# Talking-heads attention and two expert layers on one core: the raw mixing weights are cleared by VectorE and loaded first

## The chip, the cores and the metric

The kernel runs on one core of a Trainium2 chip. The metric is device microseconds from start to end of one execution; a lower number is better. A core has five engines that take their instructions in order, each from its own list: TensorE (PE; its weight loads are shown apart as PEld), VectorE (DVE), ScalarE (ACT), GpSimd (POOL) and SyncE (SP). In this kernel transfers are issued by SP and, for a few, by ACT; the transfer engines behind them are shared.

## The reference

Three stages follow each other. Only the first one is near the change.

```python
# q, k, v: 4 x 12 x 448 x 64; w_pre, w_post: 12 x 12
scores = scale * np.matmul(q, k.transpose(0, 1, 3, 2))
scores = np.einsum('bhij,hg->bgij', scores, w_pre)      # mixes the 12 heads
attn = softmax(scores)
attn = np.einsum('bhij,hg->bgij', attn, w_post)         # mixes them again
attn_out = np.matmul(attn, v)
# then: x of 1792 x 768; h = x @ w_in; x = (h - tanh(h)) @ w_out
# then: a soft mixture of 8 experts with 4 slots each, weights w1 and w2
```

## The kernel before, in words

**Attention.** Four batches are cut into chunks of at most 120 query rows, 16 chunks in all, and each chunk into slots of up to 10 query rows, which are worked on two at a time. For a chunk, PE transposes q, multiplies it by the transposed keys of each pair of heads (`sc`, line 283), ACT and DVE copy the scores to a tile `S`, and SP regroups them by a transfer `D<-S` (line 308) so that the 12 heads of 10 query rows lie on the partitions. One matmul by the block matrix `wpre` (line 317) mixes the heads. Exponentials, sums, the second mixing (line 360) by a scaled copy of the block matrix `wpost` and the product with v (line 399) follow. The later layers begin when attention ends.

**The order of the work.** It is written out by hand: every engine gets its instructions in the order in which the program names them, and only the waits between engines are added. Before the loop over slots there is a prologue. SP loads the six pairs of heads of k for the first batch (`kn`, line 166) and the first chunks of q (`qn`, line 179). PE spends the wait on ten matmuls on the identity (`warm`, line 538). Then for each pair of heads p, PE transposes k to `kx` (line 240), ACT rounds it to `khi` (line 245), DVE computes the remainder `klo` (line 249), and from p = 2 on PE does the scores of pair p - 2. Two buffers hold `kx`, so the transposes of pair p + 2 wait for `klo` of pair p. The first q is treated alike (`qx`, `qT`, lines 262 to 266).

**The mixing matrices.** `kron` builds `wpre` and then `wpost`. Each call clears a tile (`wprer` or `wpostr`) on GpSimd (line 184), lets ACT issue the transfers that repeat the 12 x 12 weights down the partitions (line 186: one transfer of 120 rows for `wpre`, two of 60 rows for `wpost`, rows of 48 bytes), and then has GpSimd spread them and mask them to a block diagonal (lines 196 to 211). After that GpSimd clears the edges of other tiles (lines 531 to 536).

**Transfer semaphores.** Transfers of both queues take eight completion semaphores in turn (`DMAHW0` to `DMAHW7` below). A transfer that takes a semaphore again waits until the transfer that held it before has landed.

Of the kernel before, what the change touches and what calls it, by code (L numbers as in the profile page):

```python
# [16 lines left out]
NB, NH, SEQ, HD = 4, 12, 448, 64  # L17
# [4 lines left out]
IH = 5  # L22
# [109 lines left out]
def talking_heads(tc, ident, q, k, v, w_pre, w_post, xd, box, follow):  # L132
    nc = tc.nc
# [26 lines left out]
    def load_k(b, p):  # L160
        if b:
            t = er.tile([JP, NR, 2, HD], FP32, tag="kn", name="kn", bufs=NP)
            nc.sync.dma_start(out=t, in_=k[b, 2 * p:2 * p + 2].rearrange("e (p r) d -> p r e d", r=NR))
        else:
            t = er.tile([JP, 2, NR, HD], FP32, tag="kn", name="kn", bufs=NP)
            nc.sync.dma_start(out=t, in_=k[b, 2 * p:2 * p + 2].rearrange("e (p r) d -> p e r d", r=NR))
        nat_k[b, p] = t
# [8 lines left out]
    def load_q(n):  # L176
        b, i0, ni, _ = chunks[n]
        t = er.tile([CHUNK, NH, HD], FP32, tag="qn", name="qn")
        nc.sync.dma_start(out=t[:ni], in_=q[b, :, i0:i0 + ni, :].rearrange("h p d -> p h d"))
        nat_q[n] = t  # L180

    def kron(name, w, scale, pre):
        rep = lt.tile([128, NH], FP32, tag=name + "r", name=name + "r", bufs=1)
        nc.gpsimd.memset(rep, 0.0)
        for at_row, n in ((4, 2 * IH),) if pre else ((4, IH), (68, IH)):
            nc.scalar.dma_start(
                out=rep[at_row:at_row + n * NH], in_=w.unsqueeze(0).to_broadcast([n, NH, NH]))
        if pre:
            big = lt.tile([128, 2 * IH, NH], FP32, tag="big", name="big", bufs=2)
            src = rep.unsqueeze(1).to_broadcast([128, 2 * IH, NH])  # L190
            pat = [[NH, 2 * IH], [0, NH]]
        else:
            big = lt.tile([128, 2, NH, IH], FP32, tag="big", name="big", bufs=2)
            src = rep.unsqueeze(1).unsqueeze(3).to_broadcast([128, 2, NH, IH])
            pat = [[64, 2], [0, NH], [NH, IH]]
        nc.gpsimd.tensor_scalar(out=big, in0=src, scalar1=scale, scalar2=None, op0=ALU.mult)
        nc.gpsimd.affine_select(
            out=big, in_=big, pattern=[[-z, c] for z, c in pat], compare_op=ALU.is_ge, fill=0.0, base=-4,
            channel_multiplier=1)
        nc.gpsimd.affine_select(  # L200
            out=big, in_=big, pattern=pat, compare_op=ALU.is_ge, fill=0.0, base=NH + 3, channel_multiplier=-1)
        if pre:
            m = lt.tile([128, 64], FP32, tag=name, name=name, bufs=1)
            nc.gpsimd.memset(m, 0.0)
            for x in range(2):
                nc.gpsimd.tensor_copy(
                    out=m[64 * x:64 * x + 64, 4:], in_=big[64 * x:64 * x + 64, IH * x:IH * x + IH].rearrange("p i g -> p (i g)"))
        else:
            m = lt.tile([128, NH, IH], FP32, tag=name, name=name, bufs=1)
            for x in range(2):  # L210
                nc.gpsimd.tensor_copy(out=m[64 * x:64 * x + 64], in_=big[64 * x:64 * x + 64, x])
        return m
# [214 lines left out]
    def plan(kind, s, *a):  # L427
        at.setdefault((kind, s), []).append(a)
# [16 lines left out]
    for m in range(1, NC):  # L445
        w = len(chunks[m - 1][3])
# [11 lines left out]
    for m in range(1, NC):  # L458
        if chunks[m][1] + CHUNK >= SEQ and m + 1 < NC:
            w = len(chunks[m - 1][3])  # L460
# [51 lines left out]
    for hi, lo, cost, f, a in sorted(wanted, key=lambda z: (z[0] - z[1], z[0])):  # L512
        s = min(range(lo, hi + 1), key=crowd)
        load["dma"][s] += cost
        plan("load", s, f, *a)

    load_k(0, 0)
    load_q(0)
    for p in (1, 2):
# [1 line left out]
    ds = [lt.tile([128, SEQ], FP32, tag=f"D{i}", name="D", bufs=1) for i in range(DB)]  # L521
    et = [lt.tile([128, SEQ + 64 - JH], FP32, tag=f"e{i}", name="e", bufs=1) for i in range(2 * EB)]
    vns = [lt.tile([128, NP, NR, HD], FP32, tag=f"vn{i}", name="vn", bufs=1) for i in range(3)]
    wpre = kron("wpre", w_pre, HD ** -0.5, True)
    wpost = kron("wpost", w_post, 1.0, False)
    warm = ps.tile([128, 128], FP32, tag="t", name="warm", bufs=2)

    for p in range(3, NP):
# [851 lines left out]
def fused_kernel(  # L1380
# [56 lines left out]
    with tc.manual_schedule():  # L1437
        talking_heads(
            tc, ident, q, k, v, w_pre, w_post, xd, box,
            lambda: moe_and_slots(tc, ident, xd, wi, wo, wo4, wis, (tshift, tlimit, moe2_phi, sel, sela, seld), moe2_w1, moe2_w2, out, box))  # L1440
# [29 lines left out]
```

## Time and profile before

| | us |
|---|---|
| median of 3 runs | 914.09 |
| lowest and highest | 909.67 and 916.29 |
| the profiled execution | 910.57 |
| span in its profile, first to last instruction | 908.8 |

| engine | busy us | share of the span |
|---|---|---|
| PE | 830.0 | 91% |
| ACT | 573.5 | 63% |
| DVE | 559.3 | 62% |
| POOL | 256.6 | 28% |

The profile is of one execution. Busy time is an average over stages that have different limits, so a stage is read by the view that follows the chain of waits back from the last instruction. Times are counted from the first instruction. The granted clock is a share of TensorE's full speed: 1.00 is 2.4 GHz and 0.50 is 1.2 GHz.

### The profile page before, as it was taken

How to read it: one execution, taken by the hardware profiler on the slowest of the kernel's cores; microseconds unless marked ns; L12 is line 12 of the kernel's file. 1: busy time of each engine (PE TensorE's matmuls, PEld its weight loads, DVE VectorE, ACT ScalarE, POOL GpSimd, SP SyncE). 2: the span in 40 equal slices, each digit the busy share in tenths (PEclk: the TensorE clock that was granted, in tenths of full speed). 3: DMA queues.
4: the chain of work that ended last, by engine and by line, in shares of the span. 5: the costliest groups of instructions: out<-in, count | busy, mean ns of one | idle time of the engine just before them, and what ended most of it. 6: DMA issues, size and time to landing. Idle time of an engine off the chain costs nothing.

```text
span 908.8 us, 28664 instructions
## 1 busy us (share of the span) xinstructions
PE 830.0 (91%) x11750; PEld 591.5 (65%) x11750; DVE 559.3 (62%) x1183; ACT 573.5 (63%) x1351; POOL 256.6 (28%) x440
## 2 busy tenths in 40 slices
PE   7868999889998899889979999999999999999995
PEld 5535676566765667666668777767776776875553
DVE  2446878668787687877445566657766777740104
ACT  2756888668877688888656676546664666731113
POOL 5334345434454344544302322000000015600000
PEclk8989999999999999999989999999999999998998
DMA  5699898897989878885648968578854435979998
GB/s 110 177 210 226 239 234 247 227 243 218 243 244 228 243 229 240 250 242 189 195 169 279 329 225 273 213 300 327 310 208 174 155 124 194 324 313 425 426 372 308
DMA packets 145910, 224.53 MB, mean 247 GB/s; under 512 B 60852, under 2 KB 127476, under 8 KB 142196
## 3 DMA queue, kind: packets, MB, share of 16 engines
q1 hardware_dynamic: 142432, 209.83, 73.8%
q10 hardware_dynamic: 3348, 12.87, 3.6%
q8 instruction: 93, 1.52, 0.7%
q14 instruction: 37, 0.30, 0.1%
HBM read 147.96 MB, written 36.18 MB: 203 GB/s over the span
## 4 chain that ended last, share of the span: by engine, by line
PE 68%; DMA 12%; ACT 8%; DVE 6%; issue 3%; POOL 1%; SPq 1%; ACTq 0%; POOLq 0%; DVEq 0%
PE hp L813 25%; DMA D<-S 9%; PE pm L317 7%; PE sc L283 6%; PE vx L399 6%; PE tm L360 6%; DVE mx L321 3%; ACT e L329 3%; PE h L1255 3%; PE gt L884 3%; PE so L1296 2%; PE tz L1275 2%; DMA rg<-wi 2%; PE lgp L934 2%; PE sp L1016 1%
## 5 line engine op out<-in xcount | busy, mean ns | idle before, releaser
L329 ACT ACTIVATE e<-pm,mx 128x448 f32<-128x448 f32 x184 | 115.1, 631 | 87.8 <-DVE mx L321 85.6
L360 PEld LDWEIGHTS tm<-wk,e 64*64 64x64 f32 x5888 | 118.2, 137 | 61.5 <-issue 37.9
L813 PE MATMUL hp<-xa,rg 128*128 128x512 f32 x576 | 152.4, 404 | 0.0
L321 DVE TENSOR_REDUCE mx<-pm 128x1 f32<-128x448 f32 x184 | 106.0, 617 | 68.8 <-PE pm L317 68.6
L360 PE MATMUL tm<-wk,e 64*64 64x60 f32 x5888 | 127.3, 223 | 17.8 <-issue 10.3
L317 PE MATMUL pm<-D,wpre 64*64 64x448 f32 (+2 forms) x736 | 119.2, 570 | 20.1 <-DMA D<-S 15.9
L813 PEld LDWEIGHTS hp<-xa,rg 128*128 128x128 f32 x576 | 102.4, 188 | 28.6 <-issue 10.8
L291 ACT ACTIVATE S<-sc 120x448 f32<-120x448 f32 (+1 forms) x186 | 91.4, 551 | 10.5 <-PE sc L283 6.6
L346 POOL TENSOR_SCALAR wk<-wpost,rv 128x60 f32<-128x60 f32 x184 | 88.4, 502 | 16.6 <-DVE rv L339 13.4
L283 PE MATMUL sc<-khi,qT 64*120 64x448 f32 (+1 forms) x384 | 84.6, 396 | 7.7 <-DVE xs L409 5.2
L775 POOL TENSOR_TENSOR rg<-rg 128x384 fp32r<-128x384 f32 x32 | 32.0, 1011 | 205.9 <-DVE rg L772 192.0
L335 POOL TENSOR_SCALAR rv<-ss 128x2 f32<-128x2 f32 x92 | 26.0, 283 | 225.0 <-ACT e L329 185.4
L399 PE MATMUL vx<-aT,vn 128*64 128x120 f32 (+1 forms) x1536 | 85.9, 266 | 0.5 <-issue 0.4
L844 DVE SCALAR_TENSOR_TENSOR qd<-qd,sq 128x512 f32<-128x512 f32 (+1 forms) x62 | 38.3, 618 | 69.8 <-ACT mk L840 63.3
L399 PEld LDWEIGHTS vx<-aT,vn 128*64 128x64 f32 x1536 | 75.6, 139 | 6.9 <-issue 2.8
L833 ACT ACTIVATE sq<-hp 128x512 f32<-128x512 f32 (+1 forms) x62 | 32.8, 530 | 71.9 <-PE hp L813 71.9
L374 ACT ACTIVATE aT<-tm 128x480 f32<-128x480 f32 x144 | 75.8, 593 | 0.2 <-PE tm L360 0.2
L813 PE MATMUL hp<-xb,rg 128*128 128x512 f32 x288 | 74.7, 404 | 0.0
L70 POOL TENSOR_TENSOR fa<-fa,f 128x384 f32<-128x384 f32 x64 | 67.3, 1052 | 9.7 <-DVE rv L339 3.6
L317 PEld LDWEIGHTS pm<-D,wpre 64*64 64x64 f32 (+2 forms) x736 | 26.3, 132 | 61.8 <-DMA D<-S 24.6
L813 PEld LDWEIGHTS hp<-xb,rg 128*128 128x128 f32 x288 | 52.0, 188 | 16.6 <-issue 6.3
L283 PEld LDWEIGHTS sc<-khi,qT 64*120 64x120 f32 (+1 forms) x384 | 46.5, 175 | 25.0 <-PE tm L360 7.4
(185 smaller groups left out, 1394.2 us busy)
## 6 DMA issues: line engine op xcount, KB each, us to landing
ex<-in_moe_w_dram SPq DMA_DIRECT2D x25, 1536.0 KB
D<-S SPq DMA_DIRECT2D x144, 210.0 KB
rg<-wis SPq DMA_DIRECT2D x32, 768.0 KB
f<-in_moe_w_in_dram SPq DMA_DIRECT2D x32, 384.0 KB
f<-in_moe_w_out_dram SPq DMA_DIRECT2D x32, 384.0 KB
wis<-rg ACTq DMA_DIRECT2D x16, 768.0 KB
rg<-wi SPq DMA_DIRECT2D x26, 384.0 KB
wi<-fa SPq DMA_DIRECT2D x32, 192.0 KB
```

What stands on the lines that cost most here:

```text
L70: eng.tensor_tensor(out=out, in0=bits(a), in1=bits(p), op=ALU.add)
L283: nc.tensor.matmul(xs[e][0][:ni], lhsT=qT[n][s, l, p, :ni], rhs=kt[s], start=(i == 0), stop=(i == 2))
L291: nc.scalar.activation(out=dst, in_=xs[e][0][:ni], func=ACTF.Copy)
L317: nc.tensor.matmul(xs[x][64 * i:64 * i + 64], lhsT=wpre[k0:k1], rhs=d[i][k0:k1], start=True, stop=True)
L321: nc.vector.tensor_reduce(out=mx[:, x:x + 1], in_=xs[x], op=ALU.max, axis=AX.X, negate=True)
L329: nc.scalar.activation(out=es[x][:, :SEQ], in_=xs[x], func=ACTF.Exp, bias=mx[:, x:x + 1], accum_out=ss[:, x:x + 1])
L346: nc.gpsimd.tensor_scalar(out=wk, in0=wpost, scalar1=rv[:, x:x + 1], scalar2=None, op0=ALU.mult)
L360: nc.tensor.matmul(xs[i][64 * z:64 * z + 64, x, c], lhsT=es[x][h, j:j + 64], rhs=wks[x][h], start=True, stop=True)
L374: nc.scalar.activation(out=out[:, :, c0:c0 + m].rearrange("p a (x i) -> p a x i", x=2), in_=x, func=ACTF.Copy)
L399: nc.tensor.matmul(x[64 * e:64 * e + 64, i, :ni], lhsT=nat_v[b, h // NP][:, h % NP, c, :], rhs=a[:, c, h, :ni], start=(c == 0), stop=(c == ...
L813: nc.tensor.matmul(hp, lhsT=r32(w[:, m, hl, cs]), rhs=r32(x_of(b, c, l)), start=(c == 0 and i == 0), stop=(c == KD - 1 and i == 2))
L844: nc.vector.scalar_tensor_tensor(out=qd, in0=qd, scalar=TG_E, in1=sq, op0=ALU.add, op1=ALU.mult)
```

## The change: the raw weights are cleared by VectorE and loaded first

`kron` is split. A new function `rows_of` allocates and clears the tile, now on VectorE, and issues the transfers on ACT. It is called for both weights ahead of the first load of k. The rest of `kron` stays where it was, and takes the filled tile. Line numbers after the split are 3 to 5 higher.

```diff
-    def kron(name, w, scale, pre):
+    def rows_of(name, w, parts):
         rep = lt.tile([128, NH], FP32, tag=name + "r", name=name + "r", bufs=1)
-        nc.gpsimd.memset(rep, 0.0)
-        for at_row, n in ((4, 2 * IH),) if pre else ((4, IH), (68, IH)):
+        nc.vector.memset(rep, 0.0)
+        for at_row, n in parts:
             nc.scalar.dma_start(
                 out=rep[at_row:at_row + n * NH], in_=w.unsqueeze(0).to_broadcast([n, NH, NH]))
+        return rep
+
+    def kron(name, rep, scale, pre):
         if pre:
...
+    pre_rows = rows_of("wpre", w_pre, ((4, 2 * IH),))
+    post_rows = rows_of("wpost", w_post, ((4, IH), (68, IH)))
     load_k(0, 0)
     load_q(0)
...
-    wpre = kron("wpre", w_pre, HD ** -0.5, True)
-    wpost = kron("wpost", w_post, 1.0, False)
+    wpre = kron("wpre", pre_rows, HD ** -0.5, True)
+    wpost = kron("wpost", post_rows, 1.0, False)
```

On ACT, the first rows of its list with what each waits for, before:

```order
L186 DMA wprer_147<-in_w_pre_dram 120x1x12 [waits Pool_49]
L186 DMA wpostr_158<-in_w_post_dram 60x1x12 [waits DMAHW1_49,Pool_49]
L186 DMA wpostr_158<-in_w_post_dram 60x1x12 [waits DMAHW2_49]
L245 ACT_TABLE_LOAD
L245 ACTIVATE khi_213<-kx_204 128x448 [waits PE_49]
L263 ACTIVATE qT_217<-qx_218 128x360 [waits PE_49]
```

and with the change:

```order
L186 DMA wprer<-in_w_pre_dram 120x1x12 [waits DVE_49]
L186 DMA wpostr<-in_w_post_dram 60x1x12 [waits DVE_49]
L186 DMA wpostr<-in_w_post_dram 60x1x12
L248 ACT_TABLE_LOAD
L248 ACTIVATE khi<-kx 128x448 [waits PE_49]
L266 ACTIVATE qT<-qx 128x360 [waits PE_49]
```

The order on ACT is the same; what its second and third transfer wait for is another: VectorE's clearing instead of GpSimd's, and no landing of an earlier transfer.

On GpSimd, the piece from the identity to the second block matrix, before:

```order
masks.py:199 AFFINE_SELECT ident<-ident 128x128
L196 TENSOR_SCALAR big<-wprer 128x120
L197 AFFINE_SELECT big<-big 128x120
L200 AFFINE_SELECT big<-big 128x120
L204 MEMSET wpre 128x64
L206 COPY wpre<-big 64x60 x2
L184 MEMSET wpostr 128x12
L196 TENSOR_SCALAR big<-wpostr 128x120
```

and with the change:

```order
masks.py:199 AFFINE_SELECT ident<-ident 128x128
L199 TENSOR_SCALAR big<-wprer 128x120
L200 AFFINE_SELECT big<-big 128x120
L203 AFFINE_SELECT big<-big 128x120
L207 MEMSET wpre 128x64
L209 COPY wpre<-big 64x60 x2
L199 TENSOR_SCALAR big<-wpostr 128x120
```

The clearing of `wpostr`, which stood behind the whole making of `wpre`, is gone from GpSimd's list.

On SP, the loads of the prologue with their waits, before:

```order
L166 DMA kn<-in_k_dram 112x2x256
L179 DMA qn<-in_q_dram 120x12x64
L166 DMA kn<-in_k_dram 112x2x256 x5
L179 DMA qn<-in_q_dram 120x12x64 [waits DMAHW0_49]
L179 DMA qn<-in_q_dram 120x12x64 [waits DMAHW3_49,DMAHW2_49,PE_49]
```

and with the change:

```order
L166 DMA kn<-in_k_dram 112x2x256
L179 DMA qn<-in_q_dram 120x12x64
L166 DMA kn<-in_k_dram 112x2x256 x3
L166 DMA kn<-in_k_dram 112x2x256 [waits DMAHW0_49]
L166 DMA kn<-in_k_dram 112x2x256 [waits DMAHW1_49]
L179 DMA qn<-in_q_dram 120x12x64 [waits DMAHW2_49]
L179 DMA qn<-in_q_dram 120x12x64 [waits DMAHW3_49,PE_49]
```

SP's order is the same. The weights' three transfers now hold semaphores 1, 2 and 4 early, so the fifth load of k waits for the landing of the first (semaphore 0), the sixth for that of `wprer` (1), and the second load of q for that of the first `wpostr` transfer (2).

## Rows read from the trace of the kernel before

**Rows 1.** Page, part 4: the whole chain of waits, shares by engine.

```profile
PE 68%; DMA 12%; ACT 8%; DVE 6%; issue 3%; POOL 1%; SPq 1%; ACTq 0%; POOLq 0%; DVEq 0%
```

**Rows 2.** Chain of waits, first 30 us: start us, us, what.

```profile
1.08 5.49 DMA wprer<-in_w_pre_dram
...
8.83 0.12 POOL wpostr L184
...
8.96 0.76 ACTq L186
...
9.77 0.74 ACTq L186
...
10.54 1.28 ACT L245
...
11.84 0.55 ACT khi L245
...
12.41 0.64 DVE klo L249
...
13.09 1.76 PE kx L240 x16
...
26.25 2.95 DMA D<-S
```

**Rows 3.** Timeline, 0 to 45 us: start, duration, engine, instruction [idle before, releaser].

```profile
0.94 0.11 POOL L184 MEMSET wprer<- 128x12 f32 x1
1.08 1.45 ACTq L186 DMA_DIRECT2D wprer<-in_w_pre_dram  x1
4.41 15.85 SPq L179 DMA_DIRECT2D qn<-in_q_dram  x2
5.96 0.99 PE L240 MATMUL kx<-ident,kn 112*64 112x112 f32 x16
6.88 0.53 PE L262 MATMUL qx<-ident,qn 120*128 120x120 f32 x3
7.33 0.77 PEld L240 LDWEIGHTS kx<-ident,kn 112*64 112x64 f32 x16 [0.15 <-DMA kn<-in_k_dram]
7.33 0.99 PE L240 MATMUL kx<-ident,kn 112*64 112x112 f32 x16
12.54 0.51 POOL L196 TENSOR_SCALAR big<-wpostr 128x120 f32<-128x120 f32 x1 [3.60 <-DMA wpostr<-in_w_post_dram]
16.19 1.76 PE L240 MATMUL kx<-ident,kn 112*64 112x112 f32 x16
19.28 0.61 PE L262 MATMUL qx<-ident,qn 120*128 120x120 f32 x3
19.83 0.99 PE L240 MATMUL kx<-ident,kn 112*64 112x112 f32 x16
21.82 0.99 PE L240 MATMUL kx<-ident,kn 112*64 112x112 f32 x16
33.33 0.23 POOL L335 TENSOR_SCALAR rv<-ss 128x2 f32<-128x2 f32 x1 [7.02 <-ACT e L329]
33.59 0.17 DVE L339 RECIPROCAL rv<-rv 128x2 f32<-128x2 f32 x1 [1.20 <-POOL rv L335]
```

**Rows 4.** Windows by stage: us, busy of PE, PEld, DVE, ACT, POOL, granted clock, DMA share, GB/s.

```profile
13.09:19.28 6.19, 6.19 (x44) 4.40 (x44) 2.79 (x5) 1.72 (x4) 5.80 (x12) 0.50 0.01 3
19.28:26.25 6.97, 6.95 (x67) 4.83 (x65) 4.63 (x8) 4.51 (x9) 6.71 (x11) 0.98 0.25 53
45.49:84.00 38.51, 26.41 (x539) 17.17 (x531) 18.87 (x45) 22.32 (x58) 13.39 (x30) 0.91 0.93 213
```

**Rows 5.** Windows of one microsecond, same columns.

```profile
7.00:8.00 1.00, 1.00 (x17) 0.84 (x19) 0.00 (x0) 0.00 (x0) 0.86 (x3) 1.00 1.12 286
10.00:11.00 1.00, 0.00 (x0) 0.00 (x0) 0.00 (x0) 0.46 (x1) 0.00 (x0) 1.00 1.27 167
```

**Rows 6.** Chain of waits, 44 to 140 us: its longest piece.

```profile
45.49 10.42 DMA D<-S
```

## The prediction, made before the changed kernel had run

> **What bounds the kernel now.** I read the chain of waits first. Over the whole span it lies on PE for 68% and on transfers for 12% [rows 1], so no small step on GpSimd or ACT matters by its busy time; one matters only where the chain itself runs through it. The first 30 us are such a place [rows 2]. The chain starts at the transfer of `wprer` (5.49 us), goes through GpSimd's making of `wpre`, then its clearing of `wpostr` at 8.83, then ACT's issue of the two `wpostr` transfers (0.76 and 0.74 us), and only then reaches ACT's table load at 10.54 and the first `khi` at 11.84. None of that is work that `khi` needs. ACT takes its list in order, and two issues stand in front of `khi` that wait for GpSimd.
>
> What `khi` does need is shown by the timeline [rows 3]: the transposes of the first k pair run from 5.96 for 0.99 us, so they end at 6.95. From there to 11.84 PE's result lies unread. PE does the first q and the second k pair (7.33, 0.99 us, to 8.32), has no buffer left, and stands until the first `klo` is written: the third pair starts at 13.09 [rows 2].
>
> The idle time has a second price. The windows by stage [rows 4] show a granted clock of 0.50, that is 1.2 GHz, from 13.09 to 19.28, directly behind those 4.8 us without a matmul, and 0.98 from 19.28 on. The transposes of a pair took 0.99 us before the gap, 1.76 at 16.19, and 0.99 again at 19.83 [rows 3].
>
> **The change, part by part.**
>
> *Clearing on VectorE.* Two memsets of 128x12 are removed from GpSimd (0.11 us each [rows 3]) and added ahead of VectorE's first work. The trace has no VectorE memset; its price lies between GpSimd's 0.11 and the 0.17 of the smallest VectorE operation, a reciprocal of 128x2 [rows 3]. VectorE first works at 12.41 in the trace [rows 2], so both are covered, and the first issue on ACT can go at about the 1.08 it goes now. On the path: 0. If VectorE started half a microsecond later, ACT would still have room, as the next item shows.
>
> *ACT's issues.* 1.45 us for `wprer` from 1.08, then 0.76 and 0.74 for `wpostr` at once: done by about 4.1. The table load (1.28) waits for nothing in ACT's list, so it is done by about 5.4. The first `khi` can then start when its transposes end, 6.95, with 1.5 us to spare. The covers are PE's warming matmuls and the transposes; were they gone, these 1.5 us are what could still be lost.
>
> *PE's third pair.* `khi` 0.55, `klo` 0.64 [rows 2]: from 6.97 to about 8.2. PE is free at 8.32, so PE decides: the third pair can start near 8.4 instead of 13.09. **Term 1: 4.7 us gained.** Lower end: rows of the third k pair must have landed. The second landed just before 7.33 (PE waited 0.15 us for it [rows 3]), and k rows then come at 286 GB/s [rows 5], so a pair of 229 KB (112 x 2 rows of 1 KB) takes 0.8 us: the third is there at about 8.1. It is nearly just in time.
>
> *More rows ahead of k.* The 120 rows of `wpostr` now move while k moves. At 286 GB/s, rows of 1 KB pass at 279 per us; in the second with q rows of 256 B and `wpostr` it is 167 GB/s [rows 5], some 650 rows per us. So 120 rows cost 0.18 us at the one rate and 0.43 at the other. **Term 2: 0.3 us lost**, the middle. Outer bounds: 0 below (these engines may have had gaps), and above 2.0: `wprer` landed 4.0 us after its issue ended, at 6.57 among the k loads, while GpSimd could use `wpostr` 2.0 us after its issue ended at 10.51 [rows 2, 3], so sharing cost a small load 2.0 and should cost a large one less.
>
> The Trainium skill ("DMA: Bandwidth & Descriptors", Specifications) speaks against the change here: it says that transfers in pieces under 512 B stay below line rate. If each 48 B row cost what 512 B do, an estimate from that page is 61 KB or 0.2 us, and the sum below would be 6.7 instead of 6.6. The trace agrees in direction: 167 GB/s against 286 [rows 5].
>
> *SP's semaphores.* The fifth k load now waits for the first to land (before 5.96, when PE uses it), the sixth for `wprer` (6.57), both instead of being issued by 4.4 [rows 3]. Behind the sixth are the second and third q loads; the second waits for the first `wpostr` transfer, at most some 2 to 4 us after its issue ends at about 3.3. With issue at 6.6 and 3.6 us more, a generous time since the first pair took 0.81 to before 5.96 with the q load beside it, the sixth is there near 10.5. It is needed two full-clock pitches and a q step after 12.7, at about 15. The third q load waits for PE anyway [rows 3]. Price: 0; the slack of 4.5 us is the cover.
>
> *The clock.* With the third pair at 8.4 PE has no gap of microseconds any more. Then two pitches from pair to pair that now take 3.10 (13.09 to 16.19) and 3.09 (to 19.28) should take the 1.99 of 19.83 to 21.82 [rows 2, 3]. **Term 3: 2.2 us gained.** Lower end 0 (the clock falls all the same).
>
> *GpSimd's list.* `wpost` is ready by about 11 instead of 14.8, and the clearings behind it end at about 22 instead of 26.3 (33.33 less the idle 7.02 [rows 3]). Their first reader comes at 33.33 less the gain, near 26.7, so they stay covered by 4 us. Price 0.
>
> *What follows.* The first `D<-S` goes at 26.25 minus the gain [rows 2]. All later loads stand behind it in SP's list, so they move with it.
>
> Sum: 4.7 - 0.3 + 2.2 = **6.6 us**. Against the profiled execution's own 910.57 (span 908.8) that is 904.0; that execution lies 3.5 below the median of the three runs, and from the median, 914.09, it is **907.5 us**.
>
> **The rivals.**
>
> *A. The clock falls all the same.* PE would still wait a little in each pair for `klo` and for banks. For it: the clock was 0.50 for 6 us although PE counted as busy throughout [rows 4]. Against it: 19.28 to 26.25 has the same instructions and gaps and kept 0.98. Gain 4.4, time 909.7. The Trainium skill ("TensorE: Matmul & The Clock Gate", A second HAM failure mode) says that small idle spells between matmul groups can make the clock swing; that is this rival, and the stretch from 19.28 does not bear it out.
>
> *B. The slots absorb it.* From 45.49 to 84 transfers are busy for 0.93 [rows 4], and one `D<-S` took 10.42 us from issue on [rows 6]. If the transfers were limited there by something that does not move, most of the gain would end in that wait: 0 to 2 us left, 912 to 914.1. Against it: those transfers are issued behind the first `D<-S`, and nothing in the stretch has a fixed time.
>
> *C. Slower: SP stands on the new semaphore.* Place: the sixth k load behind the landing of `wprer`. Point: it costs nothing until the sixth pair comes later than PE takes it now, 21.82; with 0.5 us of issue and 3.6 of transfer, `wprer` would have to land after 17.7, and each further microsecond then costs one. If it took four times its 5.49 us, landing at 23.0, the loss is 5.3 us and the time 919.4. For it: the small load already takes 5.49 us for 5.6 KB. Against it: it is first in its queue as before.
>
> *D. The change does not act*: excluded as far as order goes, since the two issues now wait for VectorE only.
>
> **Chances.** Forecast 0.62, A 0.18, B 0.15, C 0.05. The range goes from the lowest run with terms 1 and 3 whole, 909.67 - 6.9 = 902.8, to the median with no gain, 914.1; that leaves out C, half of B's upper end with the runs' own spread, and the luckiest part of the forecast. One per cent, about what a measurement of this kernel can tell, is 9.1 us: below 905.0 is faster. The forecast reaches that only with the spread of the runs: 0.18. Slower by over 1%, above 923.2, is C at its worst: 0.03. Within 1%: 0.79.
>
> **What would show it.** In the changed trace: ACT's three issues done by about 4.1, the table load before 6; the first `khi` at 7.0 (term 1); the third pair of transposes at 8.4 to 9.0 (term 2); a granted clock of 1.00 from there to the first `D<-S` and pitches of 2.0 us (term 3); that first `D<-S` near 19.6 instead of 26.25. The forecast is wrong if `khi` is early and `D<-S` is not, or if `D<-S` is 6.6 early and the end of attention is not.

## The result, and the profile after

The changed kernel takes 903.8 us (median of 4 runs, 902.0 to 907.99) against 915.19 us for the kernel before (median of 4 runs, 909.67 to 917.23). The ratio is 0.9886, with a 95% interval of 0.9846 to 0.9926. In the profiled executions the span fell from 908.8 to 901.1 us, by 7.7. Each ratio here and below leaves out the runs that were more than 1.5% above the fastest run of the same kernel.

The timeline of the changed kernel, in the same columns as [rows 3], from the first clearing to the first regrouping (`...` marks rows left out):

```profile
0.88 0.07 DVE L184 MEMSET wprer<- 128x12 f32 x1 [0.88 <-PEq L1459]
0.91 0.07 DVE L184 MEMSET wpostr<- 128x12 f32 x1
0.98 1.43 ACTq L186 DMA_DIRECT2D wprer<-in_w_pre_dram  x1
...
2.45 1.54 ACTq L186 DMA_DIRECT2D wpostr<-in_w_post_dram  x2
4.02 1.28 ACT L248 ACT_TABLE_LOAD   x1 [4.02 <-issue]
...
5.99 0.99 PE L243 MATMUL kx<-ident,kn 112*64 112x112 f32 x16
...
7.03 0.54 ACT L248 ACTIVATE khi<-kx 128x448 fp32r<-128x448 f32 x1 [1.72 <-PE kx L243]
...
7.60 0.62 DVE L252 TENSOR_TENSOR klo<-kx,khi 128x448 fp32r<-128x448 f32 x1 [6.63 <-ACT khi L248]
...
7.64 1.96 PE L243 MATMUL kx<-ident,kn 112*64 112x112 f32 x32 [0.20 <-DMA kn<-in_k_dram]
...
8.59 0.80 PEld L243 LDWEIGHTS kx<-ident,kn 112*64 112x64 f32 x16 [0.17 <-issue]
...
9.69 0.52 POOL L199 TENSOR_SCALAR big<-wpostr 128x120 f32<-128x120 f32 x1 [0.90 <-DMA wpostr<-in_w_post_dram]
...
10.33 0.99 PE L243 MATMUL kx<-ident,kn 112*64 112x112 f32 x16
...
12.05 0.53 PE L265 MATMUL qx<-ident,qn 120*128 120x120 f32 x3
...
14.50 0.77 PEld L243 LDWEIGHTS kx<-ident,kn 112*64 112x64 f32 x16 [0.31 <-issue]
...
18.91 5.98 SPq L311 DMA_DIRECT2D D<-S  x7
```

ACT's three issues end at 4.0 instead of 10.5 [rows 2], the table load is over by 5.3, and `khi` starts at 7.03 and waits there for its transposes alone. The row with 32 matmuls at 7.64 is the second and the third k pair without a gap; the weight load of the third starts at 8.59, where the row before had 13.09. The first `D<-S` goes at 18.91 instead of 26.25: 7.34 us earlier.

The windows by stage of the changed kernel, in the columns of [rows 4], cut where the same steps begin (third pair, second half of the first q, first `D<-S`):

```profile
8.59:12.05 3.46, 3.46 (x46) 2.50 (x44) 1.97 (x5) 2.18 (x4) 2.24 (x7) 1.00 1.12 195
12.05:18.91 6.86, 6.84 (x67) 4.74 (x65) 5.04 (x9) 4.44 (x9) 6.64 (x10) 1.00 0.27 55
```

The first of them took 6.19 us at a granted clock of 0.50 before, and the second 6.97 at 0.98 [rows 4].

In its first 30 us the chain of waits of the changed kernel no longer passes the weights at all. Its first long pieces are:

```profile
1.80 5.80 DMA kn<-in_k_dram
...
7.64 1.96 PE kx L243 x32
```

SP's own waits, up to 30 us, with the sum, the count and the longest:

```profile
SPq L166 <- DMA wprer<-in_w_pre_dram: 2.3, 1, 2.3
SPq L179 <- DMA wpostr<-in_w_post_dram: 1.5, 1, 1.5
...
SPq L166 <- DMA kn<-in_k_dram: 0.4, 1, 0.4
```

These are the new waits on semaphores: SP stands 2.3 us for `wprer` before the sixth k load and 1.5 for `wpostr` before the next q load. The row at 14.50 above is the sixth pair: PE's weight load waits for no transfer there.

How far the 7.3 us came can be read from the first and last start of PE's work in each later stage. Of the kernel before (engine, tile, count, ns, first to last start, forms):

```profile
L317 PE MATMUL pm<-D,wpre x736: 536/558/1006, 29.3 to 452.3; 64*64 64x448 f32 x151, 60*64 60x448 f32 x30, 48*64 48x448 f32 x2, 36*64 36x448 f32 x1
L813 PE MATMUL hp<-xa,rg x576: 387/393/793, 466.7 to 744.0; 128*128 128x512 f32 x192
L813 PE MATMUL hp<-xc,rg x288: 274/282/679, 744.2 to 799.3; 128*128 128x256 f32 x144
```

and of the changed one:

```profile
L320 PE MATMUL pm<-D,wpre x736: 536/557/1006, 22.0 to 444.7; 64*64 64x448 f32 x152, 60*64 60x448 f32 x29, 48*64 48x448 f32 x2, 36*64 36x448 f32 x1
L818 PE MATMUL hp<-xa,rg x576: 387/393/793, 457.6 to 734.8; 128*128 128x512 f32 x192
L818 PE MATMUL hp<-xc,rg x288: 274/282/682, 735.0 to 791.3; 128*128 128x256 f32 x144
```

The lead is 7.3 us at the first head mixing, 7.6 at the last, 9.1 at the first matmul of the next layer (`hp`), 8.0 at its last, and 7.7 at the end, by the spans. It goes through 420 us of slots, with their long waits for `D<-S`, without shrinking.

### The profile page after: what moved, and what is told of

Its sections match the earlier page's. It is cut to its first block, busy times and chain, and to the rows that moved or that the text cites. A ratio compares the mean times of both kernels' runs of the same rounds, so it can differ in the third digit from the quotient of the medians.

```text
span 901.1 us, 28664 instructions
## 1 busy us (share of the span) xinstructions
PE 828.2 (92%) x11750; PEld 591.0 (66%) x11750; DVE 558.9 (62%) x1185; ACT 574.3 (64%) x1351; POOL 257.9 (29%) x438
## 4 chain that ended last, share of the span: by engine, by line
PE 63%; DMA 19%; ACT 8%; DVE 6%; issue 3%; SPq 1%; POOL 0%; ACTq 0%; POOLq 0%; DVEq 0%
PE hp L818 25%; DMA D<-S 9%; PE pm L320 6%; PE vx L402 5%; PE sc L286 5%; PE tm L363 4%; ACT e L332 3%; DMA ex<-in_moe_w_dram 3%; PE gt L889 3%; DVE mx L324 3%; DMA xd<-xs 2%; PE lgp L939 2%; ACT S L294 2%; PE so L1301 2%; PE sp L1021 1%
## 5 line engine op out<-in xcount | busy, mean ns | idle before, releaser
L294 ACT ACTIVATE S<-sc 120x448 f32<-120x448 f32 (+1 forms) x186 | 91.4, 551 | 10.5 <-PE sc L286 5.1
```

The source lines that it names most:

```text
L294: nc.scalar.activation(out=dst, in_=xs[e][0][:ni], func=ACTF.Copy)
```

## The experiments

The theory: ACT's list was held up by a clearing that stood behind unrelated work on GpSimd; freeing it brings `khi` forward by 4.8 us (11.84 to 7.03) and with it the third k pair by 4.5, keeps the clock up for another 2.7, and the whole prologue's lead reaches the end. Rivals: the place ahead of the k loads or VectorE itself is what matters; the clock has no part in it; the slots absorb a shift; something beyond the prologue gains too, since 11.4 us between the medians is more than 7.3.

**Clearing on VectorE, the calls left in place.**

```diff
-        nc.gpsimd.memset(rep, 0.0)
+        nc.vector.memset(rep, 0.0)
```

> VectorE clears the two weight tiles, but both calls stay where they were in the program. Each engine's list is then the same as in the changed kernel. Theory (what counts is that ACT's second and third issue no longer wait for GpSimd): first khi at 7.0, first D<-S at 18.9, time as the changed kernel's, ratio 0.985 to 0.993. Rival (the place ahead of the k loads is what helps): issues later than 4.1, first khi nearer 11.8, ratio nearer 1.

Measured: ratio 0.9925 (0.9887 to 0.9963). In its trace ACT issues at the times of the changed kernel, with the table load right behind:

```profile
2.44 1.55 ACTq L186 DMA_DIRECT2D wpostr<-in_w_post_dram  x2
4.03 1.28 ACT L245 ACT_TABLE_LOAD   x1 [4.03 <-issue]
...
6.31 0.54 ACT L245 ACTIVATE khi<-kx 128x448 fp32r<-128x448 f32 x1 [1.00 <-PE kx L240]
...
7.38 2.07 PE L240 MATMUL kx<-ident,kn 112*64 112x112 f32 x32 [0.34 <-DMA kn<-in_k_dram]
```

`khi` is 0.7 us earlier than in the changed kernel because the ten warming matmuls took 3.92 us in this execution and 4.63 in that one. It buys little, since PE then waits for the second pair's landing. The first `D<-S` goes at 18.79. The place in the program is not needed.

**The calls moved, the clearing left on GpSimd.**

```diff
     def rows_of(name, w, parts):
...
-        nc.vector.memset(rep, 0.0)
+        nc.gpsimd.memset(rep, 0.0)
```

> Both loads are placed first, but GpSimd still clears the tiles, now both ahead of the identity's masking. Theory (GpSimd's clearing only hurt because it stood behind the making of wpre): PE's warming starts 0.1 us later, the rest as in the changed kernel: first khi at 7.1, first D<-S at 19.0, ratio 0.985 to 0.993. Rival (VectorE is needed): first khi clearly after 7.5 and a smaller gain.

Measured: first `khi` at 7.29, first `D<-S` at 18.85, ratio 0.9882 (0.983 to 0.9933). VectorE is not needed either. Each half of the change does the whole of it, because either one takes the second clearing out from behind the making of `wpre`. One more wait goes in all three kernels. In the kernel before, the first `wpostr` transfer took semaphore 1, by the order of the issues that of `wprer`, which landed at 6.57 [rows 2]. The clearing at 8.83 came later, so it is what held ACT; but had the clearing alone been taken away, the second issue could not have gone before 6.57. It goes at 2.44 to 2.54 in these kernels, so both waits are gone, and no run takes them apart.

**PE's idle time filled, in the kernel before.**

```diff
     WARM = 10
+    FILL = 10
...
     for p in range(NP):
         k_pair(0, p)()
+        if p == 1:
+            for _ in range(FILL):
+                nc.tensor.matmul(warm, lhsT=ident, rhs=ident, start=True, stop=True)
```

> The kernel before with ten more matmuls on the identity behind the second k pair, in PE's idle time from 8.32 to 13.09; nothing else is changed, so khi still starts at 11.8. Theory (part of the gain is the clock): granted clock 1.00 from 13.1 on, the third pair to the q step in 3.5 us instead of 6.19, first D<-S at 23.6 instead of 26.25, some 2.7 us faster in all, ratio 0.994 to 0.999. Rival (PE's rate there does not come from the gap): first D<-S at 26.2, ratio 1.000.

Measured: ratio 0.9959 (0.9926 to 0.9993). `khi` starts at 11.85 as before. The timeline (start, duration, idle before), and the window from the third pair to the q step in the columns of [rows 4]:

```profile
8.41 2.50 PE L544 MATMUL warm<-ident 128*128 128x128 f32 x20
13.10 0.99 PE L241 MATMUL kx<-ident,kn 112*64 112x112 f32 x16 [2.19 <-DVE klo L250]
...
23.41 5.97 SPq L309 DMA_DIRECT2D D<-S  x7
```

```profile
13.09:16.55 3.46, 3.45 (x45) 2.49 (x45) 2.21 (x5) 1.73 (x4) 2.43 (x6) 1.00 0.02 5
```

Matmuls that compute nothing shorten the next stage from 6.19 to 3.46 us, and the first `D<-S` goes at 23.41 instead of 26.25. The transposes of the third pair take 0.99 us there and no longer 1.76. So 2.73 us of the change are the clock alone, and the stage takes the same 3.46 us as in the changed kernel. The matmuls ran at 0.25 us each and left 2.19 us idle, and the clock stayed up over that.

**The prologue held back.** Two kernels, the changed one with more warming matmuls, 40 in the first (shown) and 110 in the second:

```diff
-    WARM = 10
+    WARM = 40
```

> The changed kernel with 40 warming matmuls instead of 10, which holds the whole prologue back by 30 x 0.46 = 13.8 us while the loads come at their old times. Theory (a shift of the prologue reaches the end whole): first D<-S at 32.7, the span 13.8 us longer than the changed kernel's, and 6.4 longer than the kernel before: ratio to before 1.004 to 1.010. Rival (the slots absorb a shift, half of it or more): ratio to before at or below 1.000.

Measured: first `D<-S` at 24.91, 6.0 us after the changed kernel's and not 13.8; ratio 0.9969 (0.9933 to 1.0005). My size was wrong: I took 0.46 us from the ten warming matmuls of the trace, which take twice as long as the later ones. Against its own shift, 1.34 us ahead of the kernel before, the theory gives 0.9985 and is inside the interval, but a rival that halves every shift is, too. So it was repeated with a longer lever:

> The changed kernel with 110 warming matmuls instead of 10. The run with 40 showed that those after the first few take 0.21 us, not 0.46, so the prologue starts 21 us later than in the changed kernel: first D<-S at 39.7, 13.5 us after the kernel before. Theory (a shift reaches the end whole): ratio to before 1.0147, within 1.010 to 1.019. Rival (the slots absorb half or more): 1.007 or less.

Measured: first `D<-S` at 40.16,

```profile
40.16 5.09 SPq L311 DMA_DIRECT2D D<-S  x6
```

13.91 us after the kernel before; ratio 1.0164 (1.011 to 1.0219), where 13.91 of 915 us are 1.0152. The rival's 1.007 is outside. A shift of the prologue reaches the end whole, in this direction at least.

**The changed kernel again.** No edit.

> The changed kernel once more, for its time beside the others of this series. Theory (the prologue's 7.3 us reach the end whole): ratio 0.992, and with the spread of the runs 0.988 to 0.996, so less than the 0.9886 of its first four runs. Rival (something beyond the prologue gains as well, some 4 us): ratio 0.988 or below again.

Measured: first `D<-S` at 19.06, ratio 0.9896 (0.9848 to 0.9943). It holds both the theory's 0.992 and the rival's 0.988, so alone it tells nothing apart. Set beside the shifts of all kernels, each read from one profiled execution, the excess loses much of its ground:

| kernel | first D<-S, us from 26.25 | ratio by that shift | measured |
|---|---|---|---|
| changed | -7.34 | 0.9920 | 0.9886 |
| changed, again | -7.19 | 0.9921 | 0.9896 |
| cleared on VectorE in place | -7.46 | 0.9918 | 0.9925 |
| moved only | -7.40 | 0.9919 | 0.9882 |
| filled gap | -2.84 | 0.9969 | 0.9959 |
| 40 warming matmuls | -1.34 | 0.9985 | 0.9969 |
| 110 warming matmuls | +13.91 | 1.0152 | 1.0164 |
| wpost behind k | -7.28 | 0.9920 | 0.9949 |
| split q | -8.09 | 0.9912 | 0.9929 |

The differences go both ways (-0.0037 to +0.0029) and their mean is -0.0006. The shift of the first `D<-S` is a sufficient account within what these runs can tell; whether the changed kernel gains another 0.3%, as its own two rows have it, stays open. The last row has a reason of its own, given below.

**`wpost` loaded behind k.** SP issues the two `wpost` transfers after the sixth k load.

```diff
-    def rows_of(name, w, parts):
+    def rows_of(name, w, parts, queue=nc.scalar):
...
-            nc.scalar.dma_start(
+            queue.dma_start(
...
-    post_rows = rows_of("wpost", w_post, ((4, IH), (68, IH)))
     load_k(0, 0)
...
-    wpost = kron("wpost", post_rows, 1.0, False)
...
     for p in range(3, NP):
         load_k(0, p)
+    post_rows = rows_of("wpost", w_post, ((4, IH), (68, IH)), nc.sync)
+    wpost = kron("wpost", post_rows, 1.0, False)
```

> The changed kernel with the wpost transfers issued by SP behind the last k load, so that ACT issues only wprer and no wpost row moves beside the first k pairs. Theory (term 2, the wpost rows cost the k pairs some 0.3 us): second k pair's transposes at 7.3 instead of 7.64, first D<-S at 18.6 instead of 18.91. Rival (the rows cost nothing): 7.64 and 18.9. The time moves by too little to tell either way.

Measured: the second pair's transposes wait for the same landing and start no earlier,

```profile
7.67 0.99 PE L243 MATMUL kx<-ident,kn 112*64 112x112 f32 x16 [0.24 <-DMA kn<-in_k_dram]
```

first `D<-S` at 18.97, ratio 0.9949 (0.9911 to 0.9986). No price of the 120 rows beside k is seen, but one execution of each kernel is a coarse measure: where PE waited for it, the second pair started at 7.33 (kernel before), 7.49 (filled gap) and 7.67 (here) without `wpost` rows beside it, and at 7.38 (cleared in place) and 7.64 (changed) with them. A price of 0.1 or 0.2 us would drown in that. GpSimd pays instead: it starts on `wpostr` at 11.47 rather than 9.69, and its idle time before the first `rv` shrinks to

```profile
25.93 0.23 POOL L338 TENSOR_SCALAR rv<-ss 128x2 f32<-128x2 f32 x1 [0.69 <-ACT e L332]
```

from 2.47 us in the changed kernel.

**The first q load split.** As the last one, with q's second half behind the third k pair and 7 warming matmuls. `load_q` takes heads 0 to 5 or 6 to 11 by its new second argument.

```diff
-    load_q(0)
+    load_q(0, True)
     for p in (1, 2):
         load_k(0, p)
+    load_q(0, False)
...
-    WARM = 10
+    WARM = 7
```

> As post_behind_k, and the first q chunk is loaded in two halves, the second half behind the third k pair, and there are 7 warming matmuls instead of 10. Theory (the prologue is now bound by the landing of the second and third k pair, behind 1440 q rows of 256 B): second k pair's transposes at 6.3 instead of 7.64, first D<-S at 17.5 instead of 18.9, ratio 0.0015 lower than the changed kernel's. Rival (PE's own work bounds the prologue): first D<-S not before 18.5.

Measured: first `D<-S` at 18.16, ratio 0.9929 (0.9896 to 0.9962). Half of the expected 1.4 us is there, and the time cannot be told from the changed kernel's. PE's rows say why (the window ends at 8.00, inside the last one):

```profile
4.71 1.76 PE L244 MATMUL kx<-ident,kn 112*64 112x112 f32 x16
6.40 0.66 PE L266 MATMUL qx<-ident,qn 120*128 120x120 f32 x3
7.00 1.19 PE L244 MATMUL kx<-ident,kn 112*64 112x112 f32 x20
```

The first transposes now start 1.3 us earlier, but they take 1.76 us, the time of half clock, where the changed kernel needs 0.99: after 3.3 us of warming instead of 4.6, PE was still at the lower of its two levels, judged by these durations. The second pair then waits for PE and no longer for its load. Nor does the 0.75 us of lead go further, because GpSimd is on the chain here:

```profile
25.80 0.23 POOL L339 TENSOR_SCALAR rv<-ss 128x2 f32<-128x2 f32 x1
```

The clearings, which began later as in the kernel above, ended at 25.72, so GpSimd came to the first `rv` without idle time, 0.15 us before the changed kernel's 25.95. The shift of `D<-S` therefore overstates this kernel's gain in the table.

## Why the prediction came out as it did

The forecast was 907.5 us, a gain of 6.6; the medians differ by 11.4, the spans of the profiled executions by 7.7, and the ratio's interval stands for 6.8 to 14.1 us. The direction, the place and the mechanism were as stated: ACT's list, the early third pair, the clock and the whole shift at the end each show in a row or a run. The size of the time was less sure. The median of 903.8 lies 1.0 us above the low end of the range, and below the 905.0 to which the prediction gave 0.18. In the second series the changed kernel's median was 907.81 us against 915.71, close to the forecast. Which of the two comes out depends on the spread of the runs.

- *Clearing on VectorE, path 0.* Right in that it costs nothing: the first issue goes at 0.98. The price itself, 0.07 us each, lies outside the bounds of 0.11 and 0.17, and 0.17 was not VectorE's smallest operation: a copy of 128x1 takes 0.14 in the same trace.
- *ACT's issues and the table load.* Right: done at 4.0 and 5.3 for 4.1 and 5.4.
- *Term 1, 4.7 us, and term 2, 0.3 lost.* The third pair came 4.50 us earlier, net 4.4 forecast. That it fits to 0.1 is in part chance. Term 2 is not shown: in the five executions in which PE waited for the second pair it got it between 7.33 and 7.67, with no order by whether `wpost` rows moved beside it, so a price of up to about 0.2 us cannot be excluded and none is seen. The estimate of 0.2 us from the Trainium skill ("DMA: Bandwidth & Descriptors", Specifications) is as large as this spread, so no run here shows it or refutes it.
- *Term 3, 2.2 us.* The mechanism is shown by the filled gap; the size was 2.73. I took the pitch of 1.99 from the fifth to the sixth pair; from the third to the fourth it is 1.74 (8.59 to 10.33), and 1.72 on to the q step. On the chain of the changed kernel the score matmuls behind the third and fourth pair take 0.79 and 0.81 us and those behind the fifth 1.07; why these are longer no row says. This term was mis-sized by 0.5 us, the largest part of the 0.7 that the sum missed at the first `D<-S`; 0.1 is in terms 1 and 2, and 0.1 in the stage behind (6.97 to 6.86).
- *Rival A, the clock falls all the same.* Refuted: the granted clock is 1.00 from 8.59 to 18.91, and the transposes keep their 0.99 us there, as at 10.33. The rule cited from the Trainium skill ("TensorE: Matmul & The Clock Gate", A second HAM failure mode), that small idle spells can make the clock swing, is not seen in this stretch, where PE counts as busy for 10.30 of 10.32 us; it may hold for looser ones.
- *Rival B, the slots absorb it.* Refuted for a delay by 110 warming matmuls, and for this gain by the lead of 7.3 to 9.1 us in every later stage. On the chain of the changed kernel one `D<-S` in the slots takes 9.05 us (from 38.27) and the next 10.59 (from 48.67); they moved with the rest.
- *Rival C, SP's semaphores.* The wait is real, 2.3 us at the sixth k load, issued at 6.60 as forecast. It costs nothing: PE takes that pair at 14.50, 7.9 us after the issue began, without waiting for it. When it landed, and so how much slack is left, no row shows.
- *GpSimd's list.* Its cover is smaller than I wrote: 2.47 us of idle time before the first `rv`, not 4, because its work began with `wpostr` at 9.69 and the clearings ended at 23.5, not 22. With `wpost` loaded behind k it is 0.69, and with q split as well it is gone.

The time itself lies 3.7 us under the forecast. Of these 0.7 are the sum's own miss; the rest, 3.0, is within what medians of four runs can differ by, as the runs spread over 6 us (changed) and 8 us (before). That nothing else gained is likely by the table above and not shown.

## What to carry to other kernels

An engine's list is also a queue for the transfers that it issues: look what stands in front of the first piece of work on the chain, and whether its waits belong to that work. Here either of two edits was a cure, because each took the clearing out from behind unrelated work, so ask which dependency is cut, not where the code went. Ask also what comes next: with 0.75 us more of lead, GpSimd's clearings were the limit. A gap on PE may cost more than its length, and a cheap test is to fill it with matmuls that compute nothing; but a price for such filler must come from rows at the clock that it will run at.

## What the runs showed of the hardware beside this

The granted clock in the windows reads 1.00 from the first microsecond, yet PE's first matmuls are slow. In the kernel with 40 warming matmuls, windows of 2 us show 12 passes of the same matmul, then 15, then 21 (ten matmuls on the identity are 20 rows of the trace, so two passes each):

```profile
2.00:4.00 2.00, 2.00 (x12) 2.00 (x11) 0.00 (x0) 0.00 (x0) 0.00 (x0) 1.00 0.89 219
4.00:6.00 2.00, 2.00 (x15) 2.00 (x15) 0.00 (x0) 1.28 (x1) 0.00 (x0) 1.00 1.06 224
6.00:8.00 2.00, 2.00 (x21) 2.00 (x20) 0.00 (x0) 0.00 (x0) 1.58 (x6) 1.00 1.13 248
```

So in these traces the number does not show the slow start, and the durations have to be read; in the kernel with q split it reads 1.00 as well while the transposes take 1.76 us. When PE gets faster also differs between executions: the same first transposes took 0.99 us in one profiled execution of the changed kernel and 1.44 in the other.
